# Gate, up and down products as unsplit fp32 matmuls in an attention and GEGLU kernel

## The chip, the cores and the metric

The kernel runs on one core of a Trainium2 chip. The metric is the device time of one execution, in microseconds (us); lower is better. Nothing else runs on the chip.

## What is computed

The input x has 2048 rows (tokens) of 576 columns. Its layer norm xn feeds two branches, self-attention with 32 heads of 18 columns, and a GEGLU feed-forward block with 4608 hidden columns; their outputs are multiplied, and x is added:

```python
xn = layernorm(x)
s  = attention(xn, wqkv, wo)                        # 32 heads, Dh = 18, softmax over 2048 keys
g  = silu((gelu(xn @ w_gate) * (xn @ w_up)) @ w_down)   # F = 4608, gelu with tanh
out = x + s * g
```

All inputs and the output are fp32.

## The kernel before, in words

**Numbers.** TensorE (PE) takes two kinds of 32-bit operand here: F32, and F32R, a 32-bit format that has been rounded. Every product but one is made with F32R operands. Where a product needs more than one rounded operand holds, each fp32 operand is cut in two: a high part (the rounded value) and a low part (the rest). A product is then three matmuls that add up in one PSUM bank: high by high, low by high, high by low. The one exception is the product of the softmax weights with the values (`values`, L764), whose operands are F32 and not split.

**Tiling of the feed-forward block.** The tokens go in NB = 4 blocks of 512, the hidden columns in 36 tiles of 128. One *section* (`section`, L533) is one token block by one hidden tile; there are NF = 144 of them. A section makes the transposed gate values `pg` and up values `pu`, each 128 hidden columns by 512 tokens, in one PSUM bank each. The 576 input columns are contracted in NC = 9 chunks of 64. Partitions 0 to 63 of the weight tile hold the gate weights, 64 to 127 the up weights, and the transposed xn (`xd`) lies twice, once in each half. So `pair` (L409) issues one matmul for `pg` in the upper 64 rows of the array and one for `pu` in the lower 64 rows, and there are 9 x 3 = 27 such pairs in a section (`terms`, L407).

**Activation.** `activate` (L423) makes gelu(pg) * pu: Square on ScalarE (ACT), a multiply on VectorE (DVE), a copy of `pu` to `t2` on ACT and `t2 * pg` on DVE (`times`), then tanh on ACT and (tanh + 1) * t2 on DVE (`rest`, L440). The last 6 sections (`early` false) use a shorter form without `t2`.

**Splits.** GpSimd (POOL) splits the weights of the next section, in three pieces of 128x384 (`split_gu`, L129), with `split` (L105: a tensor_scalar for the high part, a tensor_tensor for the low part). `finish` (L577) splits the hidden values into `hh` and `hl` and, in every second section, the w_down rows into `dh` and `dl`. In the first ten sections ACT makes the high part (`split_ap`), in the last six ACT and DVE split (`cut`). The transposed xn is split once, in `split_t` (L185), stored to DRAM as two arrays (`xhs`, L249), and loaded as `xd` (L142), after which POOL copies it to the other half of the partitions (L146).

**Down product.** Two hidden tiles (G = 2) make one *block* of the down product: 8 sums (4 token tiles of 128, by 2 column halves of 288), each over 256 hidden columns, that DVE adds to `Y` (`add_down`, L448). There are 72 blocks. In most of them (`half_downs`, L474) each 128-row product is cut into two halves of 64 rows; the rows 0 to 63 and 64 to 127 of the array work on different sums, and each half is one matmul of 64 rows (`down_product`, L463, L465), 6 terms per sum and half. The other blocks use 128 rows at once.

**Attention and the order of the work.** The order of PE's instructions is written out by hand (`manual_schedule` for PE); the other engines' are arranged by a scheduler, within the order of each tile's uses. Attention is cut into 32 units of 4 heads by 512 queries. In sections 10 to 137 the 27 gate and up pairs are interleaved (`spread`) with 16 pairs of attention matmuls: one score matmul `pe` (L729, then Exp on ACT, L730) and one matmul `pm` (L698) of a later unit for the row maximum (L699, DVE). Both have 64 rows, and the two of a pair take the two halves of the array. After every second section comes a burst of the value products (L764: 8 key tiles by 4 heads, 128 rows by 32 columns each, the four heads in the array's four column strips), and after the others a down block. Before the sections stand the layer norm, its transposes, and the query, key and value projections (L180, 128 rows, F32R, three terms); after section 137 the output projection (L902) runs with the last six sections.

Of the kernel before, what the change touches and what calls it, by code (L numbers as in the profile page):

```python
# [17 lines left out]
P = 128  # L18
# [29 lines left out]
BANKS = {"f": 2, "m": 3, "s": 3}  # L48
EPS = 1e-5
# [20 lines left out]
def kernel(ctx: ExitStack, tc: tile.TileContext, x, wqkv, wo, w_gate, w_up, w_down, out):  # L70
# [19 lines left out]
    xhs = [dram.tile([2, D, TB], F32, name=f"xhs{b}") for b in range(NB)]  # L90
# [28 lines left out]
    def raw_tile(shape, pool=wts):  # L119
        return pool.tile(shape, F32, name="raw", tag="raw", bufs=2)  # L120

    def load_gu(t, keep=lambda i: i):

        raw = raw_tile([P, NC, P])
        for a, w in enumerate((w_gate, w_up)):
            keep(nc.sync.dma_start(raw[HR * a:HR * a + HR], w[:, t * P:(t + 1) * P].rearrange("(k p) n -> p k n", p=HR)))
        return raw, [], []

    def split_gu(w, k, keep=lambda i: i):  # L129
        hi, lo = (wts.tile([P, XG, P], F32R, name=m, bufs=5) for m in ("wh", "wl"))  # L130
        first = split(hi, lo, w[0][:, XG * k:XG * k + XG, :], keep)
        w[1].append(hi)
        w[2].append(lo)
        return first

    def load_xd(b, key=None):

        xd = [[], []]
        for c in range(0, NC, XG):
            for i in range(2):  # L140
                t = wts.tile([P, XG, TB], F32R, name=f"xd{i}_{c}")
                asked[:] = [nc.sync.dma_start(f(t)[0:HR], xhs[b][i, c * HR:(c + XG) * HR, :]  # L142
                                              .rearrange("(k p) t -> p k t", p=HR))]
                if key:
                    no_sync(asked[0], key, "keys first")
                copied[:] = [nc.gpsimd.tensor_copy(t[HR:P], t[0:HR])]  # L146
                xd[i].append(t)
        return xd
# [8 lines left out]
    with tc.tile_pool(name="pro", bufs=1) as pro, tc.tile_pool(name="pps", bufs=1, space=PSUM) as pps:  # L157
# [27 lines left out]
        def split_t(pt, k, xt):  # L185

            if k < KT:
                nc.scalar.activation(xt[0][:, k, :], pt, AF.Copy)
# [45 lines left out]
        def transposes(b, xr):  # L234
            xt = XT[b % 2]
            pts = [pps.tile([P, TB], F32, name="pt", bufs=KT + 1) for k in range(KT + 1)]
            for j in range(4):
                if b == 0 and j == 0:
                    warm(46)
                for k in range(KT + 1):  # L240
                    nc.tensor.transpose(pts[k][:, j * P:(j + 1) * P], xr[j][:, k * P:(k + 1) * P], ident)  # L241
            for k in range(KT + 1):
                split_t(pts[k], k, xt)
            return xt

        def store_xt(b, xt):
            keep = tc.keep_in_program_order if b == 0 else lambda i: i
            for i in range(2):
                keep(nc.sync.dma_start(xhs[b][i, 0:R0, :].rearrange("(k p) t -> p k t", p=P), f(xt[i])))  # L249
                keep(nc.sync.dma_start(xhs[b][i, R0:D, :], f(xt[2])[HR * i:HR * i + HR, :]))  # L250
# [96 lines left out]
        for b in range(NB):  # L347
# [29 lines left out]
            if b == 2:  # L377
                ahead = load_gu(0, tc.keep_in_program_order)
                for k in range(NG):
                    split_gu(ahead, k)  # L380
# [22 lines left out]
    def gate_up(tag):  # L403

        w, xd = FF["w"], FF["xd"]
        pg, pu = (ps.tile([P, TB], F32, name=n, tag=tag, bufs=BANKS[tag]) for n in ("pg", "pu"))
        terms = [(wp, *divmod(c, XG), xp) for c in range(NC) for wp, xp in ((0, 0), (1, 0), (0, 1))]  # L407

        def pair(i):  # L409
            wp, k, c, xp = terms[i]  # L410
            for a, o in enumerate((pg, pu)):
                rr = slice(HR * a, HR * a + HR)
                nc.tensor.matmul(o, w[1 + wp][k][rr, c, :], xd[xp][k][rr, c, :], start=(i == 0),  # L413
                                 stop=(i == len(terms) - 1))

        return [lambda i=i: pair(i) for i in range(len(terms))], pg, pu
# [6 lines left out]
    def activate(pg, pu, early):  # L423

        t1 = ffn.tile([P, TB], F32, name="t1", bufs=2)
# [10 lines left out]
        def rest(behind=None, evicted=None):  # L436
            tanh = kept(nc.scalar.activation(t1, t1, AF.Tanh, scale=GC * GS))
            if behind:
                no_sync(tanh, behind, "a mark first")
            one = kept(nc.vector.scalar_tensor_tensor(t1, t1, 1.0, t2 if early else pg, op0=ALU.add, op1=ALU.mult))  # L440
            if evicted:
                no_sync(one, evicted, "a finished sum first")
            if not early:
                kept(nc.vector.tensor_tensor(t1, t1, pu, op=ALU.mult))
# [13 lines left out]
    DOWN = [(a, w, g) for g in range(G) for a, w in ((0, 0), (0, 1), (1, 0))]  # L458
# [4 lines left out]
    def down_product(py, hs, wd, j, c, i, rr=slice(0, P), start=False, stop=False):  # L463
        a, w, g = DOWN[i]
        return nc.tensor.matmul(py, hs[g][a][rr, j * P:(j + 1) * P], wd[w][rr, g, 288 * c:288 * c + 288],  # L465
                                start=start, stop=stop)
# [7 lines left out]
    def half_downs(b, r, hs, wd, Y):  # L474
# [9 lines left out]
        def downs_of(a, ks):  # L484
            for k in ks:
                for i in range(m):
                    def step(k=k, i=i):
# [6 lines left out]
                        one = down_product(pys[k], hs, wd, j, c, i, slice(HR * a, HR * a + HR), fresh,  # L494
                                           begun == 0 and i == m - 1)
                        if begun == 0 and i == 0 and k in seen:
                            after(one, seen[k])
# [31 lines left out]
    def load_down(r, raw):  # L529
        kept(nc.sync.dma_start(raw, w_down[r * G * P:(r + 1) * G * P, :].rearrange("(g p) n -> p g n", p=P)))  # L530
        return raw

    def section(specials=(), tag="f", raw_d=None, ahead=True):  # L533
# [17 lines left out]
        if nxt:  # L551
            for k in range(NG - 1 if ahead else 0):
                first = split_gu(nxt, k, kept)
                if k == 0 and n in ATT and n > ATT.start:
                    no_sync(first, FF["hl"], "hidden values first")
        if g == G - 1:
            FF["rawd"] = load_down(r, raw_d() if raw_d else raw_tile([P, G, D])) if ahead else FF.pop("next_d")
        for p in spread(pairs, specials):
            p()
        if nxt and ahead:  # L560
            split_gu(nxt, NG - 1, kept)
# [15 lines left out]
    def finish(pool=ffn, cut=split, bufs=1):  # L577
# [6 lines left out]
        if n in ATT and copied:  # L584
            no_sync(first, copied.pop(), "transposed x first")
        FF["hl"] = low_part[0]
        FF["hs"].append((hh, hl))
        if n % G == G - 1:
            wd = [pool.tile([P, G, D], F32R, name=m, bufs=bufs) for m in ("dh", "dl")]
            cut(*wd, FF["rawd"])  # L590
            for h in range(2):
                once = n in ATT and n + G in ATT
                FF["down"].append((b, r, FF["hs"], wd, FF["Y"], (2 * h, 2 * h + 1), once, n + 1 + (0 if once else h)))
# [51 lines left out]
    with tc.tile_pool(name="att", bufs=1, reuse_waits="tile") as att:  # L645
# [155 lines left out]
        def lead_raw():  # L801
            t = att.tile([P, QD, TB], F32, name="pT", bufs=8)
            return t.rearrange("p a t -> p (a t)")[:, 0:G * D].rearrange("p (g d) -> p g d", g=G)

# [7 lines left out]
        for n, m in enumerate(FIRST):  # L812
            none = [lambda: None]
            lead = [lambda s=s: lead_pair(s) for s in range(slot, slot + m)]
            section((n == 2) * 5 * none + lead + (m > 0 and n != 2) * none, "s" if n == 1 else "f", lead_raw)
# [12 lines left out]
            finish(cut=split_ap)  # L828
# [28 lines left out]
    with tc.tile_pool(name="epi", bufs=1, reuse_waits="tile") as epi:  # L857
# [57 lines left out]
        def cut(hi, lo, raw):  # L915
            split_av(hi, lo, raw, kept)

# [11 lines left out]
        def next_weights(n):  # L929


            if n + 2 < ENDS:
                FF["next_gu"] = load_gu((len(FIRST) + n + 2) % (NR * G), kept)
            if n % G == 0:
                FF["next_d"] = load_down((len(FIRST) + n) // G % NR, epi.tile([P, G, D], F32, name="raw", tag="raw"))

        done = 0
        for n in range(NU * NA, ENDS):
# [23 lines left out]
            else:  # L962
                next_weights(n)
                for k in range(0 if last else NG - 1):
                    split_gu(FF["w"], k, kept)
            downs()
            run_rest()
            if first or last:
                finish(epi, cut, 2)
            else:  # L970
                for i in range(3):
# [6 lines left out]
                    if i == 0:  # L978
                        split_gu(FF["w"], NG - 1, kept)
                    prepare(done - 1 + AHEAD)  # L980
                    if i == 1:
                        finish(epi, cut, 2)
# [59 lines left out]
```

## Time and profile before

| what | us |
|---|---|
| median of 3 runs | 2548.07 (2547.3 to 2548.31) |
| span of the profiled execution | 2545.4 |
| median less that span | 2.7 |
| PE busy | 2538.4 |
| DVE busy | 1950.4 |
| ACT busy | 1555.1 |
| POOL busy | 1320.7 |

The span runs from the first to the last recorded instruction. PE in the profile is TensorE's matmuls, PEld its weight loads, which run beside them. A matmul's record lasts until its last result has come out, so the records of matmuls that follow one another overlap, and so do those of two matmuls in the two halves of the array: the pace of PE is read from the distance of the starts, not from the length of a record. `x2592` in a row is the number of records.

### The profile page before, as it was taken

Reading aid. Unit: us, or ns where it says so; the run is one execution under the profiler, and the core shown is the slowest. Engines: PE = TensorE matmul, PEld = TensorE weight load, DVE = VectorE, ACT = ScalarE, POOL = GpSimd, SP = SyncE. Lnnn points to the kernel's source line nnn. Section 1 sums busy time; section 2 is a strip of 40 time slices with the busy share of each in tenths; the row PEclk is TensorE's granted clock in tenths of the full one; section 3 lists DMA queues with packets and bytes.
Section 4 is the critical chain, followed back from the end, with each engine's and each line's share of the span. In section 5 each row is a group of like instructions: output and inputs, shape, how many; then the busy total and the mean of one; then the engine's idle time right before and its main releaser. Section 6 shows DMA issues by size and latency. Waiting matters only on the chain.

```text
span 2545.4 us, 63167 instructions
## 1 busy us (share of the span) xinstructions
PE 2538.4 (100%) x23974; PEld 2008.4 (79%) x23974; DVE 1950.4 (77%) x3499; ACT 1555.1 (61%) x3050; POOL 1320.7 (52%) x1447
## 2 busy tenths in 40 slices
PE   9999999999999999999999999999999999999999
PEld 8888877777777777777777787777777777787798
DVE  5316988888888888888888888888888888887277
ACT  3223366666677666676666677666676666676612
POOL 2117545555465554445565545554446555455675
PEclk9999999999999999999999999999999999999999
DMA  8876444444465444444455444444446444444483
GB/s 267 269 241 158 100 103 106 100 111 109 107 150 121 104 109 112 113 112 110 111 125 140 116 111 106 105 108 112 109 109 153 115 109 109 108 106 99 114 242 107
DMA packets 398686, 325.51 MB, mean 128 GB/s; under 512 B 117408, under 2 KB 309184, under 8 KB 398384
## 3 DMA queue, kind: packets, MB, share of 16 engines
q1 hardware_dynamic: 398384, 321.47, 49.7%
q8 instruction: 191, 3.13, 0.5%
q14 instruction: 111, 0.91, 0.1%
HBM read 266.63 MB, written 54.70 MB: 126 GB/s over the span
## 4 chain that ended last, share of the span: by engine, by line
PE 98%; ACT 1%; DVE 0%; DMA 0%; SPq 0%; issue 0%; ACTq 0%
PE pg L413 29%; PE py L465 18%; PE acc L764 18%; PE pm L698 9%; PE pe L729 9%; PE po L180 7%; PE pu L413 6%; PE po L902 2%; ACT pT L730 1%; PE pt L241 0%; SPq L665 0%; DMA xx<-in_A_x_dram 0%; DVE bs L209 0%; ACT t L426 0%; DMA KS<-qk 0%
## 5 line engine op out<-in xcount | busy, mean ns | idle before, releaser
L730 ACT ACTIVATE pT<-pe 128x512 f32<-128x512 f32 x2048 | 1153.3, 598 | 368.7 <-PE pm L698 226.3
L699 DVE TENSOR_REDUCE mx<-pm 128x1 f32<-128x512 f32 x2048 | 1249.6, 680 | 151.3 <-PE pm L698 149.0
L413 PE MATMUL pg<-xd,wh 64*128 64x512 f32 x2592 | 928.9, 390 | 0.0
L413 PE MATMUL pu<-xd,wh 64*128 64x512 f32 x2592 | 928.6, 390 | 0.0
L698 PE MATMUL pm<-KS,q 64*128 64x512 f32 x2048 | 779.0, 388 | 0.8 <-DMA KS<-qk 0.5
L729 PE MATMUL pe<-q,KS 64*128 64x512 f32 x2048 | 775.2, 387 | 0.0
L413 PEld LDWEIGHTS pg<-xd,wh 64*128 64x128 f32 x2592 | 476.5, 184 | 115.9 <-POOL wh L106 21.1
L413 PE MATMUL pg<-xd,wl 64*128 64x512 f32 x1296 | 501.6, 387 | 0.0
L413 PE MATMUL pu<-xd,wl 64*128 64x512 f32 x1296 | 501.4, 387 | 0.0
L413 PEld LDWEIGHTS pu<-xd,wh 64*128 64x128 f32 x2592 | 477.0, 184 | 2.0
L764 PE MATMUL acc<-pT,VS 128*32 128x512 f32 x4096 | 452.8, 594 | 0.0
L108 POOL TENSOR_TENSOR wl<-raw,wh 128x384 fp32r<-128x384 f32 x432 | 434.2, 1019 | 13.7
L106 POOL TENSOR_SCALAR hh<-t 128x512 fp32r<-128x512 f32 x128 | 79.1, 618 | 652.0 <-DVE t L440 637.8
L698 PEld LDWEIGHTS pm<-KS,q 64*128 64x128 f32 x2048 | 374.2, 184 | 31.1 <-DVE mx L699 4.3
L729 PEld LDWEIGHTS pe<-q,KS 64*128 64x128 f32 x2048 | 370.9, 184 | 21.9
L465 PE MATMUL py<-dh,hh 64*128 64x288 f32 (+1 forms) x2160 | 360.3, 294 | 0.3
L465 PE MATMUL py<-dl,hh 64*128 64x288 f32 (+1 forms) x2160 | 358.7, 292 | 0.0
L465 PE MATMUL py<-dh,hl 64*128 64x288 f32 (+1 forms) x2160 | 358.3, 292 | 0.0
L764 PEld LDWEIGHTS acc<-pT,VS 128*32 128x32 f32 x4096 | 127.4, 110 | 289.9 <-issue 278.0
L106 POOL TENSOR_SCALAR wh<-raw 128x384 fp32r<-128x384 f32 x432 | 217.2, 515 | 143.7 <-PE pu L413 83.4
L453 DVE TENSOR_TENSOR Y<-py,Y 128x288 f32<-128x288 f32 x544 | 227.1, 452 | 59.8 <-PE py L465 52.7
L413 PEld LDWEIGHTS pg<-xd,wl 64*128 64x128 f32 x1296 | 238.7, 184 | 32.1
(119 smaller groups left out, 3106.7 us busy)
## 6 DMA issues: line engine op xcount, KB each, us to landing
KS<-qk SPq DMA_DIRECT2D x1536, 36.0 KB
raw<-in_B_w_gate_dram SPq DMA_DIRECT2D x144, 288.0 KB
raw<-in_B_w_up_dram SPq DMA_DIRECT2D x144, 288.0 KB
raw<-in_B_w_down_dram SPq DMA_DIRECT2D x67, 576.0 KB
VS<-vs SPq DMA_DIRECT2D x128, 152.0 KB
qk<-t SPq DMA_DIRECT2D x72, 256.0 KB
q<-qk SPq DMA_DIRECT2D x384, 36.0 KB
xx<-in_A_x_dram SPq DMA_DIRECT2D x32, 288.0 KB
```

Of the source, the lines that this page charges most:

```text
L106: first = nc.gpsimd.tensor_scalar(hi, raw, 1.0, 1.0, op0=ALU.mult, op1=ALU.mult)
L108: low_part[:] = [keep(nc.gpsimd.tensor_tensor(lo, raw, f(hi), op=ALU.subtract))]
L180: nc.tensor.matmul(o, st, m, start=(i == 0), stop=(i == len(terms) - 1))
L413: nc.tensor.matmul(o, w[1 + wp][k][rr, c, :], xd[xp][k][rr, c, :], start=(i == 0), stop=(i == len(terms) - 1))
L453: one = kept(nc.vector.tensor_tensor(yy, py, yy, op=ALU.add))
L465: return nc.tensor.matmul(py, hs[g][a][rr, j * P:(j + 1) * P], wd[w][rr, g, 288 * c:288 * c + 288], start=start, stop=stop)
L698: nc.tensor.matmul(pm, QS[u, r][rr, t * P:(t + 1) * P], KS[(u * NA + c) % KB][r][rr, :], start=True, stop=True)
L699: nc.vector.tensor_reduce(MX[u][:, 2 * r + a, t, c:c + 1], pm, axis=AX.X, op=ALU.max)
L729: nc.tensor.matmul(pe, KS[(u * NA + c) % KB][r][rr, t * P:(t + 1) * P], QS[u, r][rr, :], start=True, stop=True)
L730: nc.scalar.activation(PT[u, kt][:, 2 * r + a, :], pe, AF.Exp, scale=SCALE)
L764: nc.tensor.matmul(ACC[u][32 * a:32 * a + 32, :], VS[(u * NA + c) % VB][:, v:v + 32], pt[:, a, :], start=first, stop=last, skip_group_chec ...
L902: nc.tensor.matmul(po, parts_of(b, j)[x_][:, k, :], OW[w][c][k], start=(i == 0), stop=(i == len(OUT) - 1))
```

## The change

The operands of the gate, up and down products are no longer split. The weights are loaded as fp32 (`gu`, three buffers, and `wd`, three buffers) and used as they are; the hidden values go from the activation (`t1`, now four buffers) to the down product; the transposed xn is kept whole, in a third copy that ACT makes in the prologue (`xf`), stored to DRAM as one array and loaded as `xd`. Each product that was three matmuls with F32R operands is one matmul with F32 operands, of the same 64 rows, 128 stationary columns and 512 or 288 moving columns. The loops over `CW` have one pass, since `CW` is 128. The gelu of sections 0 to 137 ends on POOL, in two instructions, where it ended on DVE in one. Some orders written by hand that belonged to the splits go. Attention and the projections keep their F32R operands and splits.

```diff
+CW = P
-    xhs = [dram.tile([2, D, TB], F32, name=f"xhs{b}") for b in range(NB)]
+    xhs = [dram.tile([D, TB], F32, name=f"xhs{b}") for b in range(NB)]
...
     def load_gu(t, keep=lambda i: i):
-        raw = raw_tile([P, NC, P])
+        t_ = wts.tile([P, NC, P], F32, name="gu", bufs=3)
...
-    def split_gu(w, k, keep=lambda i: i):
...
     def load_xd(b, key=None):
-        xd = [[], []]
+        xd = []
         for c in range(0, NC, XG):
-            for i in range(2):
-                t = wts.tile([P, XG, TB], F32R, name=f"xd{i}_{c}")
...
+            t = wts.tile([P, XG, TB], F32, name=f"xd{c}")
...
-        def split_t(pt, k, xt):
+        def split_t(pt, k, xt, xf):
+            if k < KT:
+                nc.scalar.activation(xf[:, k, :], pt, AF.Copy)
+            else:
+                nc.scalar.activation(xf[0:HR, k, :], pt[0:HR], AF.Copy)
...
+        XF = [pro.tile([P, KT + 1, TB], F32, name="xf")] * 2
...
-        terms = [(wp, *divmod(c, XG), xp) for c in range(NC) for wp, xp in ((0, 0), (1, 0), (0, 1))]
-        def pair(i):
-            wp, k, c, xp = terms[i]
-            for a, o in enumerate((pg, pu)):
-                rr = slice(HR * a, HR * a + HR)
-                nc.tensor.matmul(o, w[1 + wp][k][rr, c, :], xd[xp][k][rr, c, :], start=(i == 0),
-                                 stop=(i == len(terms) - 1))
+        def pair(c):
+            for o in range(0, P, CW):
+                for a, out_ in enumerate((pg, pu)):
+                    rr = slice(HR * a, HR * a + HR)
+                    nc.tensor.matmul(out_[o:o + CW, :], w[rr, c, o:o + CW], xd[c // XG][rr, c % XG, :], start=(c == 0),
+                                     stop=(c == NC - 1), skip_group_check=True)
...
-        t1 = ffn.tile([P, TB], F32, name="t1", bufs=2)
+        t1 = ffn.tile([P, TB], F32, name="t1", bufs=G + 2)
...
-            one = kept(nc.vector.scalar_tensor_tensor(t1, t1, 1.0, t2 if early else pg, op0=ALU.add, op1=ALU.mult))
...
+            if early:
+                kept(nc.gpsimd.tensor_scalar(t1, t1, 1.0, 1.0, op0=ALU.add, op1=ALU.mult))
+                kept(nc.gpsimd.tensor_tensor(t1, t1, t2, op=ALU.mult))
+            else:
+                kept(nc.vector.scalar_tensor_tensor(t1, t1, 1.0, pg, op0=ALU.add, op1=ALU.mult))
...
-    DOWN = [(a, w, g) for g in range(G) for a, w in ((0, 0), (0, 1), (1, 0))]
+    DOWN = list(range(G))
...
-        a, w, g = DOWN[i]
-        return nc.tensor.matmul(py, hs[g][a][rr, j * P:(j + 1) * P], wd[w][rr, g, 288 * c:288 * c + 288],
-                                start=start, stop=stop)
+        for o in range(0, P, CW):
+            one = nc.tensor.matmul(py[o:o + CW, :], hs[i][rr, j * P + o:j * P + o + CW], wd[rr, i, 288 * c:288 * c + 288],
+                                   start=start, stop=stop, skip_group_check=True)
+            first = one if o == 0 else first
+        return first, one
...
-        hh = ffn.tile([P, TB], F32R, name="hh", bufs=G + 1)
-        hl = ffn.tile([P, TB], F32R, name="hl", bufs=G + 1)
-        first = cut(hh, hl, FF["act"])
...
+        FF["hs"].append(FF["act"])
         if n % G == G - 1:
-            wd = [pool.tile([P, G, D], F32R, name=m, bufs=bufs) for m in ("dh", "dl")]
-            cut(*wd, FF["rawd"])
```

More of the change, by code (lines that the diff above doesn't have):

```diff
@@ L117, in split_av, with raw_tile @@
         keep(nc.vector.tensor_tensor(lo, raw, f(hi), op=ALU.subtract))
-    def raw_tile(shape, pool=wts):
-        return pool.tile(shape, F32, name="raw", tag="raw", bufs=2)
+    def raw_tile(shape):
+        return wts.tile([P, NC, P], F32, name="gu", bufs=3).rearrange("p k n -> p (k n)")[:, 0:shape[1]]
     def load_gu(t, keep=lambda i: i):
-        raw = raw_tile([P, NC, P])
+        t_ = wts.tile([P, NC, P], F32, name="gu", bufs=3)
         for a, w in enumerate((w_gate, w_up)):
-            keep(nc.sync.dma_start(raw[HR * a:HR * a + HR], w[:, t * P:(t + 1) * P].rearrange("(k p) n -> p k n", p=HR)))
-        return raw, [], []
-    def split_gu(w, k, keep=lambda i: i):
[L130 to L134, printed above, removed]
+            keep(nc.sync.dma_start(t_[HR * a:HR * a + HR], w[:, t * P:(t + 1) * P].rearrange("(k p) n -> p k n", p=HR)))
+        return t_
     def load_xd(b, key=None):
-        xd = [[], []]
+        xd = []
         for c in range(0, NC, XG):
-            for i in range(2):
-                t = wts.tile([P, XG, TB], F32R, name=f"xd{i}_{c}")
[L142 to L147, printed above, removed]
+            t = wts.tile([P, XG, TB], F32, name=f"xd{c}")
+            asked[:] = [nc.sync.dma_start(t[0:HR], xhs[b][c * HR:(c + XG) * HR, :].rearrange("(k p) t -> p k t", p=HR))]
+            if key:
+                no_sync(asked[0], key, "keys first")
+            copied[:] = [nc.gpsimd.tensor_copy(t[HR:P], t[0:HR])]
+            xd.append(t)
         return xd
@@ L406, in gate_up @@
         pg, pu = (ps.tile([P, TB], F32, name=n, tag=tag, bufs=BANKS[tag]) for n in ("pg", "pu"))
[L407 to L416 removed]
+        def pair(c):
[4 more added lines that the diff above has]
+                                     stop=(c == NC - 1), skip_group_check=True)
+        return [lambda c=c: pair(c) for c in range(NC)], pg, pu
     def gate(o, th, yy):
@@ L493, in step @@
                         begun = a if k < low else 1 - a
-                        one = down_product(pys[k], hs, wd, j, c, i, slice(HR * a, HR * a + HR), fresh,
+                        first, one = down_product(pys[k], hs, wd, j, c, i, slice(HR * a, HR * a + HR), fresh,
                                            begun == 0 and i == m - 1)
                         if begun == 0 and i == 0 and k in seen:
-                            after(one, seen[k])
+                            after(first, seen[k])
                         if i == m - 1:
@@ L527, in down, with load_down, section @@
                 kept(nc.sync.dma_start(ys[b * TB + j * P:b * TB + (j + 1) * P, :], Y[:, j]))
[L529 to L533, printed above, removed]
+    def load_down(r):
+        wd = wts.tile([P, G, D], F32, name="wd", bufs=3)
+        kept(nc.sync.dma_start(wd, w_down[r * G * P:(r + 1) * G * P, :].rearrange("(g p) n -> p g n", p=P)))
+        return wd
+    def section(specials=(), tag="f", ahead=True):
         n = FF["n"]
@@ L551, in section @@
         if nxt:
[L552 to L555, printed above, removed]
+            pass
         if g == G - 1:
-            FF["rawd"] = load_down(r, raw_d() if raw_d else raw_tile([P, G, D])) if ahead else FF.pop("next_d")
+            FF["rawd"] = load_down(r) if ahead else FF.pop("next_d")
         for p in spread(pairs, specials):
             p()
-        if nxt and ahead:
-            split_gu(nxt, NG - 1, kept)
         FF["w"] = nxt
@@ L575, in downs, with finish @@
             down(*FF["down"].pop(0)[:-1])
-    def finish(pool=ffn, cut=split, bufs=1):
+    def finish():
         n = FF["n"] - 1
         b, r = divmod(n // G, NR)
-        hh = ffn.tile([P, TB], F32R, name="hh", bufs=G + 1)
-        hl = ffn.tile([P, TB], F32R, name="hl", bufs=G + 1)
-        first = cut(hh, hl, FF["act"])
[L584 to L587, printed above, removed]
+        FF["hs"].append(FF["act"])
         if n % G == G - 1:
-            wd = [pool.tile([P, G, D], F32R, name=m, bufs=bufs) for m in ("dh", "dl")]
-            cut(*wd, FF["rawd"])
             for h in range(2):
                 once = n in ATT and n + G in ATT
-                FF["down"].append((b, r, FF["hs"], wd, FF["Y"], (2 * h, 2 * h + 1), once, n + 1 + (0 if once else h)))
+                FF["down"].append((b, r, FF["hs"], FF["rawd"], FF["Y"], (2 * h, 2 * h + 1), once, n + 1 + (0 if once else h)))
     def load_numbers(num, rb, g, toks):
@@ L814 @@
             lead = [lambda s=s: lead_pair(s) for s in range(slot, slot + m)]
-            section((n == 2) * 5 * none + lead + (m > 0 and n != 2) * none, "s" if n == 1 else "f", lead_raw)
+            section((n == 2) * 5 * none + lead + (m > 0 and n != 2) * none, "s" if n == 1 else "f")
             if slot + m >= NS > slot:
@@ L827 @@
             downs()
-            finish(cut=split_ap)
+            finish()
         for n in range(NU * NA):
@@ L934, in next_weights @@
             if n % G == 0:
[L935 removed]
+                FF["next_d"] = load_down((len(FIRST) + n) // G % NR)
         done = 0
@@ L968 @@
             if first or last:
-                finish(epi, cut, 2)
+                finish()
             else:
```

23 lines of the change are left out of this document (4 added, 19 removed).

## The prediction, made before the changed kernel ran

> **What bounds the kernel now.** I read the page first: busy times, then the chain that ended last. In the busy rows each engine is followed by its time, its share of the span and its number of instructions; the chain gives shares of the span.
>
> ```profile
> PE 2538.4 (100%) x23974; PEld 2008.4 (79%) x23974; DVE 1950.4 (77%) x3499; ACT 1555.1 (61%) x3050; POOL 1320.7 (52%) x1447
> PE 98%; ACT 1%; DVE 0%; DMA 0%; SPq 0%; issue 0%; ACTq 0%
> ```
>
> PE is busy throughout and is 98% of the chain. Matmul records overlap, so this could still hide slack; the pace has to be read from starts. The timeline of one stretch in the middle (start, length, engine, line, operation) gives it; the cut-out rows go on in the same way:
>
> ```profile
> 1300.20 0.39 PE L729 MATMUL pe<-q,KS 64*128 64x512 f32 x1
> 1300.20 0.39 PE L698 MATMUL pm<-KS,q 64*128 64x512 f32 x1
> 1300.43 0.39 PE L413 MATMUL pg<-xd,wh 64*128 64x512 f32 x1
> 1300.43 0.39 PE L413 MATMUL pu<-xd,wh 64*128 64x512 f32 x1
> ...
> 1307.00 0.39 PE L413 MATMUL pg<-xd,wh 64*128 64x512 f32 x1
> 1307.00 0.39 PE L413 MATMUL pu<-xd,wh 64*128 64x512 f32 x1
> 1307.23 0.29 PE L465 MATMUL py<-dh,hh 64*128 64x288 f32 x2
> ...
> 1312.00 0.29 PE L465 MATMUL py<-dh,hh 64*128 64x288 f32 x2
> ```
>
> Two matmuls of 64 rows start together, one in each half of the array. From 1300.20 to 1307.23 there are 31 such starts: 7.03 / 31 = **0.227 us per pair** with 512 moving columns. From 1307.23 to 1312.00 there are 36 steps: 4.77 / 36 = **0.1325 us per pair** with 288. Starts follow without holes, so here PE works at its own pace; neither ACT nor DVE holds it up.
>
> Now the counts, from the groups (records, then busy and mean ns; the other two terms of each down form have the same counts):
>
> ```profile
> L413 PE MATMUL pg<-xd,wh 64*128 64x512 f32 x2592 | 928.9, 390 | 0.0
> L413 PE MATMUL pg<-xd,wl 64*128 64x512 f32 x1296 | 501.6, 387 | 0.0
> L465 PE MATMUL py<-dh,hh 64*128 64x288 f32 x2016 | 315.8, 293 | 0.2
> L465 PE MATMUL py<-dh,hh 128*128 128x288 f32 x144 | 44.5, 309 | 0.1
> L764 PE MATMUL acc<-pT,VS 128*32 128x512 f32 x4096 | 452.8, 594 | 0.0
> ```
>
> Gate and up: 2592 + 1296 = 3888 pairs x 0.227 = 883 us. Down in halves: 3 x 2016 = 6048 matmuls, 3024 pairs x 0.1325 = 401 us. Down with 128 rows, which I take at the same pace (mean 309 against 293 ns): 432 x 0.1325 = 57 us. These 1341 us are what the change touches, and PE is the bound in all of it.
>
> **What an unsplit fp32 matmul costs: the term that decides.** The trace has one product of this kind, the value products at L764. The program has 32 units x 16 key tiles x 4 heads = 2048 of them, and the trace 4096 records: each fp32 matmul is *two* records, each with a weight load of its own. One burst:
>
> ```profile
> 1323.47 7.07 PE L764 MATMUL acc<-pT,VS 128*32 128x512 f32 x64
> ```
>
> It holds 64 records = 16 sets of four (four heads, in four column strips side by side). The last set ends 0.59 us after its start (mean of the row above), so a set takes (7.07 - 0.59) / 15 = **0.432 us**, close to twice a pair of the F32R kind (0.227). A record is thus two passes over its 512 columns and a matmul four, 2 x 0.432 = **0.864 us**, where the three F32R terms take 3 x 0.227 = **0.681 us**. One matmul for three is four passes for three.
>
> No record of 64 rows by 128 columns in fp32 exists in this trace. Bounds: below, the burst's rate, 0.864 per pair; above, four F32R passes with the F32R overhead in each, 4 x 0.227 = 0.908. I take 0.864, because the burst is the row with the same operands. For 288 columns: 0.864 x 288 / 512 = 0.486 below, 4 x 0.1325 = 0.530 above; I take 0.486.
>
> **Do the halves still work side by side?** F32R pairs do (same start above). With two records a matmul there is a new question, that of order: in the compiled program the two records of a matmul stand one directly behind the other, first `pg`'s two, then `pu`'s two. The second must wait for the first in its half. If it held up everything behind it, the four heads' eight records would come in steps, two at a time, and 64 records would take about 33 x 0.432 = 14 us. The burst took 7.07: a strip goes on by itself while another is occupied. I expect the same of row halves, but no row shows it. Here a rule speaks against me: the Trainium skill, TensorE: Matmul & The Clock Gate, section "The mechanism" (Part 3), says that matmuls start and end in program order, "strict FIFO, no reordering". By that rule the burst would have taken the 14 us; the trace's 7.07 us disagrees for column strips. For row halves it becomes a rival below.
>
> **The sum.** Pairs after: 3888 / 3 = 1296 of gate and up, 3024 / 3 = 1008 of down halves, 432 / 3 = 144 with 128 rows.
> - Gate and up: 1296 x (0.864 - 0.681) = +237 us (upper bound, 0.908: +294).
> - Down halves: 1008 x (0.486 - 0.3975) = +89 us (upper, 0.530: +134).
> - Down, 128 rows: 144 x 0.0885 = +13 us (upper +19).
> Together **+339 us**, upper bound +447.
>
> **The splits that go, and the gelu that moves.** They lie on engines off the chain:
>
> ```profile
> L108 POOL TENSOR_TENSOR wl<-raw,wh 128x384 fp32r<-128x384 f32 x432 | 434.2, 1019 | 13.7
> L106 POOL TENSOR_SCALAR wh<-raw 128x384 fp32r<-128x384 f32 x432 | 217.2, 515 | 143.7 <-PE pu L413 83.4 <-DMA raw<-in_B_w_up_dram 55.6 <-PE pm L698 3.4
> L108 POOL TENSOR_TENSOR hl<-t,hh 128x512 fp32r<-128x512 f32 x128 | 164.7, 1287 | 10.7
> L106 POOL TENSOR_SCALAR hh<-t 128x512 fp32r<-128x512 f32 x128 | 79.1, 618 | 652.0 <-DVE t L440 637.8 <-PE py L465 13.8
> L440 DVE SCALAR_TENSOR_TENSOR t<-t,t 128x512 f32<-128x512 f32 x138 | 97.3, 705 | 16.1 <-ACT t L437 2.0
> ```
>
> POOL sheds these 434 + 217 + 165 + 79 = 895 us and more, and gains 138 x (0.618 + 1.287) = 263 us by the durations of the same shapes. Nothing on the chain waits for POOL, so I cost both at 0 us. The cover is a whole section (over 10 us) between the end of a gelu and the down block that uses it; the new end takes 1.9 us where L440 and the split took 0.7 + 1.9. DVE loses L440's 97 us. One window over a whole period (two sections, a burst, a down block) shows the room; the columns are PE, PEld, DVE, ACT and POOL busy, each with its number of instructions:
>
> ```profile
> 1300.00:1333.50 33.50, 33.50 (x338) 26.00 (x336) 27.12 (x48) 23.27 (x47) 20.70 (x20) 1.00 0.71 152
> ```
>
> PE fills 33.5 of 33.5; DVE 27.1, ACT 23.3. The period grows by 18 x 0.183 + 16 x 0.0885 = 4.7 us, to 38.2, while DVE goes down to 25.7. The attention matmuls now come in bursts, two pairs (0.45 us) between two gate pairs (0.86): DVE's and ACT's share, at most two reductions or Exps of about 0.6 to 0.7 us per 1.32 us, still fits, with three banks for each. If it doesn't always, some tenths of a us per section over 128 sections, up to 40 us, are lost; the upper bound has room for it.
>
> **Prologue and DMA.** ACT makes five more copies for each token block:
>
> ```profile
> L188 ACT ACTIVATE xth<-pt 128x512 fp32r<-128x512 f32 x16 | 8.3, 604 | 2.6 <-PE pt L241 2.6
> ```
>
> 5 x 0.604 = 3 us. In the first block they stand ahead of the first projection: +3 us. In the other three they run beside the value projections on PE, whose three banks could run full: 0 to 3 us each. The single `xf` buffer makes the copies of the next block wait for the store of the last, 0 to 3 us. The end of the kernel has no split of the last hidden values: -1 us. I take +5 us in all (0 to 15). `xhs` and `xd` move half the bytes, the weights the same; SP issues fewer DMAs, and weights come a section ahead into three buffers. No chain step is a DMA: 0 us.
>
> Span 2545.4 + 339 + 5 = 2889 us. The median lay 2.7 us above the span: **2892 us**. Likeliest case with its bounds: 2870 to 3015 (+447, +15, rounded up).
>
> **Rivals.**
> 1. *Strict order between the halves.* A gate pair then takes steps: `pg` record 1 at 0, `pg` 2 and `pu` 1 at 0.432, `pu` 2 at 0.864, the attention matmul of the upper half at 0.864, that of the lower half only at 1.296, and what follows is behind it: 1.296 in place of 0.864 + 0.227 = 1.091, so +0.205 us. 9 pairs x 128 sections: +236 us; the ends of the 63 down blocks and of the other sections +20. Down pairs in a row cost nothing more. 2892 + 256 = **3148 us**. For: the program's order. Against: the burst.
> 2. *The halves take turns in fp32.* A pair costs 1.728 and a down pair 0.972: 1296 x 1.047 + 1008 x 0.5745 + 13 = +1949, **4502 us**. Against: F32R halves and fp32 strips both work side by side.
> 3. *Faster: a record of 64 rows needs one pass.* If the two passes come from the use of all 128 rows (the burst's form), a half-height matmul would cost 0.432 per pair: 1296 x (0.432 - 0.681) + 1008 x (0.243 - 0.3975) + 13 = -466, **2088 us**, with DVE (1950 - 97 = 1853 us) just below PE. It turns faster where a record costs under 0.34 us. Against: in F32R the number of rows makes little difference (mean lengths 293 and 309 ns in the two down rows above).
> 4. *The change saves waits that I don't see.* PE's starts follow without holes, so there is nothing to save; a result within 0.2% would need this to cancel 340 us.
>
> **How the numbers follow.** 0.2% is about what a measurement of this kernel can tell from no change. Likeliest case 0.73; rival 1 0.16; rival 2 0.04; rival 3 0.03; rival 4 0.01; slower for another reason, between 3015 and 3400 us, 0.03. The range reaches from below the likeliest case to rival 1: 2860 to 3155. Faster 0.03, same 0.01, slower 0.96.
>
> **What would show it.** 5184 records at the gate and up line (2592 matmuls, two each), with starts 0.43 to 0.45 us apart in each half, and mean lengths near 0.59 us as in the burst; down records 0.24 to 0.27 us apart. Between a gate pair and the next attention pair 0.86 to 0.9 us, both attention matmuls starting together; under rival 1 they start 0.43 us apart. PE still 98% of the chain; POOL's busy time under 750 us. Wrong would be: a PE with holes behind POOL or ACT, or a record length near 0.39 us (one pass).

## The result, and the profile after

The changed kernel took 2888.35 us (median of 4 runs, 2885.88 to 2889.15), the one before 2547.69 us (4 runs): a ratio of 1.1334, 95% interval 1.1318 to 1.135. It is 341 us slower. The forecast was 2892 us. The profiled execution has a span of 2884.1 us, 338.7 us more than before.

From the page of the changed kernel, the busy row and the chain by engine and by line:

```profile
PE 2873.3 (100%) x19222; PEld 1673.8 (58%) x19222; DVE 1936.2 (67%) x3352; ACT 1532.4 (53%) x3046; POOL 408.0 (14%) x448
PE 99%; DMA 0%; ACT 0%; DVE 0%; issue 0%; SPq 0%
PE pg L406 38%; PE py L459 19%; PE acc L748 16%; PE pe L713 9%; PE pm L682 8%; PE po L172 6%; PE po L882 2%; PE pu L406 1%; PE pt L237 0%; DMA rawp<-in_A_wqkv_dram 0%; DMA xhs<-xf 0%; ACT xf L180 0%; ACT xth L184 0%; DMA xx<-in_A_x_dram 0%; DVE bs L205 0%; DVE t L287 0%
```

The chain by line before:

```profile
PE pg L413 29%; PE py L465 18%; PE acc L764 18%; PE pm L698 9%; PE pe L729 9%; PE po L180 7%; PE pu L413 6%; PE po L902 2%; ACT pT L730 1%; PE pt L241 0%; SPq L665 0%; DMA xx<-in_A_x_dram 0%; DVE bs L209 0%; ACT t L426 0%; DMA KS<-qk 0%
```

PE is still the whole chain. POOL went from 1320.7 to 408.0 us, and nothing of that can be seen in the time. The chain's share of `pg` and `pu` rose from 35% to 39% of a longer span, from about 890 to about 1125 us. The shares are rounded to whole per cents, so this shows where the time went and is too coarse for a sum.

The groups of PE by form, with records, busy time and mean ns:

```profile
L406 PE MATMUL pg<-xd,gu 64*128 64x512 f32 x2592 | 1307.6, 589 | 0.0
L682 PE MATMUL pm<-KS,q 64*128 64x512 f32 x2048 | 1086.5, 607 | 0.0
L459 PE MATMUL py<-wd,t 64*128 64x288 f32 x4032 | 499.2, 402 | 0.0
L748 PE MATMUL acc<-pT,VS 128*32 128x512 f32 x4096 | 452.7, 594 | 0.0
L459 PE MATMUL py<-wd,t 128*128 128x288 f32 x288 | 74.3, 412 | 0.0
```

2592 records for `pg` are 1296 matmuls with two records each, as for the value products; the mean length, 589 ns, is that of the value products (594). There were 3888 `pg` records of 390 and 387 ns before. A trap lies in the second row: the attention matmul `pm` is the same as before, when its row was

```profile
L698 PE MATMUL pm<-KS,q 64*128 64x512 f32 x2048 | 779.0, 388 | 0.8 <-DMA KS<-qk 0.5 <-DVE mx L699 0.3
```

yet its mean length rose from 388 to 607 ns. It costs no more. Its record begins while the gate matmul ahead of it in the same half still runs. (The ends of matmul records are modelled by the profiler; that is one more reason to read the pace from starts.) The timeline of one step shows it:

```profile
1300.93 0.59 PE L406 MATMUL pg<-xd,gu 64*128 64x512 f32 x1
1300.93 0.59 PE L406 MATMUL pu<-xd,gu 64*128 64x512 f32 x1
1301.35 0.59 PE L406 MATMUL pg<-xd,gu 64*128 64x512 f32 x1
1301.36 0.59 PE L406 MATMUL pu<-xd,gu 64*128 64x512 f32 x1
1301.38 0.79 PE L713 MATMUL pe<-q,KS 64*128 64x512 f32 x1
1301.38 1.02 PE L682 MATMUL pm<-KS,q 64*128 64x512 f32 x2
1302.02 0.39 PE L713 MATMUL pe<-q,KS 64*128 64x512 f32 x1
1302.25 0.59 PE L406 MATMUL pg<-xd,gu 64*128 64x512 f32 x1
1302.25 0.59 PE L406 MATMUL pu<-xd,gu 64*128 64x512 f32 x1
```

Both halves start together, twice, 0.43 us apart: two records, read as two passes each, for one pair. Then come two attention pairs, and the next gate pair starts 1.32 us after the first. That is 0.86 + 2 x 0.23, so nothing is lost between the halves. (The prediction's sign, 0.86 us from a gate pair to the attention pair, can't be read directly: the attention records begin 0.45 us after the gate pair, for the reason just given.)

A down block now has 64 records in place of 96; the second row is the next work on PE:

```profile
1512.50 7.92 PE L459 MATMUL py<-wd,t 64*128 64x288 f32 x64
1520.04 0.61 PE L713 MATMUL pe<-q,KS 64*128 64x512 f32 x1
```

32 sets of two in 7.92 us, the last 0.40 us long: (7.92 - 0.40) / 31 = 0.2426 us a set, 0.485 per pair.

The span by stage, from the starts of the first gate matmul, the first score and the last score:

| stage | before, us | after, us | difference |
|---|---|---|---|
| prologue, to the first gate matmul | 196.2 | 203.4 | +7.2 |
| first sections, to the first score | 103.6 | 122.7 | +19.1 |
| attention sections (64 periods) | 2110.2 | 2406.8 | +296.6 |
| last sections and end | 135.5 | 151.2 | +15.7 |

A period of two sections, a burst and a block went from 32.97 to 37.61 us: +4.64.

### The profile page after: what moved, and what is told of

Read it like the earlier page. It is cut to its first block, busy times and chain, and to the rows that moved or that the text cites. A ratio compares the mean times of both kernels' runs of the same rounds, so it can differ in the third digit from the quotient of the medians.

```text
span 2884.1 us, 52436 instructions
## 1 busy us (share of the span) xinstructions
PE 2873.3 (100%) x19222; PEld 1673.8 (58%) x19222; DVE 1936.2 (67%) x3352; ACT 1532.4 (53%) x3046; POOL 408.0 (14%) x448
## 4 chain that ended last, share of the span: by engine, by line
PE 99%; DMA 0%; ACT 0%; DVE 0%; issue 0%; SPq 0%
PE pg L406 38%; PE py L459 19%; PE acc L748 16%; PE pe L713 9%; PE pm L682 8%; PE po L172 6%; PE po L882 2%; PE pu L406 1%; PE pt L237 0%; DMA rawp<-in_A_wqkv_dram 0%; DMA xhs<-xf 0%; ACT xf L180 0%; ACT xth L184 0%; DMA xx<-in_A_x_dram 0%; DVE bs L205 0%; DVE t L287 0%
## 5 line engine op out<-in xcount | busy, mean ns | idle before, releaser
L406 PE MATMUL pg<-xd,gu 64*128 64x512 f32 x2592 | 1307.6, 589 | 0.0
L406 PE MATMUL pu<-xd,gu 64*128 64x512 f32 x2592 | 1306.8, 589 | 0.0
L682 PE MATMUL pm<-KS,q 64*128 64x512 f32 x2048 | 1086.5, 607 | 0.0
L713 PE MATMUL pe<-q,KS 64*128 64x512 f32 x2048 | 1081.7, 610 | 0.0
L406 PEld LDWEIGHTS pg<-xd,gu 64*128 64x128 f32 x2592 | 479.0, 186 | 181.0 <-issue 87.8
L459 PE MATMUL py<-wd,t 64*128 64x288 f32 (+1 forms) x4320 | 573.5, 403 | 0.0
L459 PEld LDWEIGHTS py<-wd,t 64*128 64x128 f32 (+1 forms) x4320 | 437.4, 187 | 153.9 <-issue 41.6
L406 PEld LDWEIGHTS pu<-xd,gu 64*128 64x128 f32 x2592 | 480.2, 186 | 1.6
L420 DVE SCALAR_TENSOR_TENSOR t<-t,pg 128x512 f32<-128x512 f32 x144 | 98.8, 686 | 140.8 <-ACT t L419 140.7
L435 POOL TENSOR_TENSOR t<-t,t 128x512 f32<-128x512 f32 x138 | 175.4, 1271 | 11.5
```

What stands on the lines that cost most here:

```text
L406: nc.tensor.matmul(out_[o:o + CW, :], w[rr, c, o:o + CW], xd[c // XG][rr, c % XG, :], start=(c == 0), stop=(c == NC - 1), skip_group_check ...
L420: kept(nc.vector.scalar_tensor_tensor(t1, t1, 1.0 / GC, pg, op0=ALU.add, op1=ALU.mult))
L435: kept(nc.gpsimd.tensor_tensor(t1, t1, t2, op=ALU.mult))
L459: one = nc.tensor.matmul(py[o:o + CW, :], hs[i][rr, j * P + o:j * P + o + CW], wd[rr, i, 288 * c:288 * c + 288], start=start, stop=stop, s ...
L682: nc.tensor.matmul(pm, QS[u, r][rr, t * P:(t + 1) * P], KS[(u * NA + c) % KB][r][rr, :], start=True, stop=True)
L713: nc.tensor.matmul(pe, KS[(u * NA + c) % KB][r][rr, t * P:(t + 1) * P], QS[u, r][rr, :], start=True, stop=True)
```

## The experiments

The theory: a product costs its passes through PE, four for an fp32 matmul against three for the three F32R terms; all else that the change moves is hidden, but for some microseconds in the prologue. The rivals: part of the 341 us is waits (POOL's longer gelu, the third copy, new buffers), or part of it is order between the halves of the array. Each run stood beside runs of the kernel before on the same chip (2547 to 2548 us in all of them).

### Gate and up alone

On the changed kernel, the down product split again:

```diff
-        FF["hs"].append(FF["act"])
+        cut(hh, hl, FF["act"])
+        FF["hs"].append((hh, hl))
...
+            cut(*wd, FF["rawd"])
...
-    DOWN = list(range(G))
+    DOWN = [(a, w, g) for g in range(G) for a, w in ((0, 0), (0, 1), (1, 0))]
```

> Gate and up unsplit as in the changed kernel, the down product split into three F32R terms as before. Theory (four passes for three, all else hidden): the changed kernel's 2888 us less the down part, 1008 x 0.0885 + 144 x 0.0885 = 102 us, so 2786 us (2775 to 2800); the splits of the hidden values after the gelu on POOL stay hidden. Rival (a part of the 340 us is not matmul passes but waits behind POOL's gelu or the new buffers): the time does not come out as that difference; with POOL's gelu and splits in one chain before the down block it would stay near 2888 us or above.

Measured: 2790.79 us (ratio to before 1.0955, 1.0938 to 1.0971), +243 us. The theory's 2786 missed by 5 us; the long chain on POOL, gelu and splits one after the other, cost no more than that.

### Down alone

On the kernel before, the hidden values and w_down unsplit:

```diff
-        FF["hs"].append((hh, hl))
+        FF["hs"].append(FF["act"])
...
-    DOWN = [(a, w, g) for g in range(G) for a, w in ((0, 0), (0, 1), (1, 0))]
+    DOWN = list(range(G))
```

> The kernel before with the down product alone unsplit; gate, up, xn and the end of the gelu as before. Theory: 2548 + 102 = 2650 us (2640 to 2660). Rival (waits): the two parts done alone, this one and gate and up alone, would not add up to the whole 340 us; if order between the halves cost something in the down blocks, this one would be over 2700 us.

Measured: 2638.95 us (1.0361, 1.0345 to 1.0376), +92 us, 10 less than worked out. The two parts give 243 + 92 = 335 of the 341 us: no large cost needs both.

### The end of the gelu back on DVE

```diff
-                kept(nc.gpsimd.tensor_scalar(t1, t1, 1.0, 1.0, op0=ALU.add, op1=ALU.mult))
-                kept(nc.gpsimd.tensor_tensor(t1, t1, t2, op=ALU.mult))
+                kept(nc.vector.scalar_tensor_tensor(t1, t1, 1.0, t2, op0=ALU.add, op1=ALU.mult))
```

> The changed kernel with the end of the gelu back on DVE, one instruction as before. Theory: POOL's two instructions were off the path and DVE has room (1936 us busy, +97): 2888 us, within 5 us. Rival (the longer end on POOL delays down blocks): faster by 10 us or more.

Measured: 2889.38 us (2886.8 to 2891.03) against 2888.35. No difference: the move to POOL neither cost nor brought anything here. The attention sections take 2406.8 us in both traces.

### No third copy of xn

```diff
-                nc.scalar.activation(xf[:, k, :], pt, AF.Copy)
...
-            keep(nc.sync.dma_start(xhs[b][0:R0, :].rearrange("(k p) t -> p k t", p=P), XF[b % 2][:, 0:KT, :]))
+            keep(nc.sync.dma_start(xhs[b][0:R0, :].rearrange("(k p) t -> p k t", p=P), f(xt[0])))
```

> The changed kernel without the third copy of xn: the high part of xn, which the projections use, is stored and loaded in its place, so the low part of xn is left out of gate and up. Theory: the copies cost about 5 us in the prologue, so 2883 us (2875 to 2887). Rival (the copies were hidden): 2888 us, no difference.

Measured: 2881.97 us (2881.27 to 2882.55), 6.4 us faster than the changed kernel by the medians. In the two traces the first gate matmul starts at 199.8 us in place of 203.4, 3.6 us earlier, and all later stages agree within 0.1 us. So the copies cost some 4 to 6 us, in the prologue.

### Four F32R terms

On the kernel before, a fourth term:

```diff
-        terms = [(wp, *divmod(c, XG), xp) for c in range(NC) for wp, xp in ((0, 0), (1, 0), (0, 1))]
+        terms = [(wp, *divmod(c, XG), xp) for c in range(NC) for wp, xp in ((0, 0), (1, 0), (0, 1), (1, 1))]
...
-    DOWN = [(a, w, g) for g in range(G) for a, w in ((0, 0), (0, 1), (1, 0))]
+    DOWN = [(a, w, g) for g in range(G) for a, w in ((0, 0), (0, 1), (1, 0), (1, 1))]
```

> The kernel before with a fourth term, low by low, in the gate, up and down products: four F32R matmuls where the changed kernel has one F32 matmul. Theory (a product costs its passes, 0.227 and 0.1325 us per F32R pair): +294 + 134 + 19 = 447 us, 2995 us (2970 to 3010), about 107 us above the changed kernel, whose passes have the smaller overhead of the value products (0.858 us per four). Rival (the price of the changed kernel is not one of passes): no such relation; near 2888 us if an F32 matmul were four F32R passes to the nanosecond.

Measured: 2983.69 us (1.1714, 1.1695 to 1.1734), +437 us where 447 were worked out. With all splits made and the order of the kernel before, a fourth F32R matmul alone costs more than the whole change. So the price of passes is enough to explain the change, and four F32R matmuls cost 95 us more than one fp32 matmul in the two kernels. That a record of an fp32 matmul is two passes is a reading of its time (0.429 us against 0.227); the trace shows records, not passes.

### Down matmuls grouped by half, two and four at a time

On the changed kernel, in `half_downs`, with K = 2 and K = 4:

```diff
-        for i, both in enumerate(zip(*rows, strict=True)):
-            for half in both if i < low * m + m else both[::-1]:
-                half()
+        for i in range(0, len(rows[0]), K):
+            for row in rows if i < low * m + m else rows[::-1]:
+                for half in row[i:i + K]:
+                    half()
```

> The changed kernel; in the down blocks two matmuls (four records) of one half are issued, then two of the other, where they alternated one by one. Theory (a half goes on by itself, records of one half do not hold up those of the other): 2888 us, within 10 us. Rival (records start in program order, so a record that waits for its own half holds up the other): a group of four takes 6 x 0.243 = 1.46 us in place of 0.97, 63 blocks x 8 groups x 0.49 = +245 us, 3130 us.

> As the run by two, but four matmuls (eight records) of one half, then four of the other. Theory: 2888 us, within 15 us, if PE can look eight records and their weight loads ahead; if its look ahead is shorter, some tenths of the rival's price. Rival (program order): 14 x 0.243 = 3.4 us per group in place of 1.94, 63 x 4 x 1.46 = +367 us, 3255 us.

Measured: by two 2901.99 us, +14 us; by four 3094.31 us (1.2147 of before), +206 us. The down records in the first two stretches of 0.97 us of a down block (length, PE busy, granted clock, DMA share and GB/s; the number behind x counts the records that run in the stretch, and in the first stretch all of them also start there), by two:

```profile
1521.28:1522.25 0.97, 0.96 (x8) 1.00 0.28 78
1522.25:1523.22 0.97, 0.97 (x11) 1.00 0.22 76
```

and by four:

```profile
1532.04:1533.01 0.97, 0.96 (x4) 1.00 0.33 112
1533.01:1533.98 0.97, 0.97 (x9) 1.00 0.19 61
```

By two, four records of the one half stand ahead of the first of the other, and still eight start in the first stretch, both halves at once. By four, eight stand ahead, and only four start: the other half begins when the fifth record of the first half does. So neither of the two theories holds alone. The halves are independent as long as few records of one stand ahead of the other: four ahead cost 14 us in all, 0.22 us for each of the 63 blocks, and eight cost 206 us, 3.3 us a block (the rival's program order: 245 and 367 us). In the changed kernel it is two. What sets the limit, records or their weight loads, was not tested.

### Fewer columns per matmul

On the changed kernel:

```diff
-CW = P
+CW = 64
```

and, in a second run, `CW = 32`.

> The changed kernel with each product as two matmuls of 64 stationary columns (64 rows by 64 columns, four corners of the array). Theory (the four corners work side by side, each with four passes): 2888 us, within 20 us. Rival (only halves of rows work side by side, or the doubled number of records costs something each): up to double, 1296 x 0.86 + 1008 x 0.49 = +1600 us.

> The changed kernel with each product as four matmuls of 32 stationary columns (eight tiles of the array). Theory (as with four column strips in the value products, at 0.43 us per record): 2888 us, within 30 us, if PE can hold 16 records and their weight loads per chunk in flight. Rival (look ahead too short, or a cost per record): slower by 7 ns or more for each of the 31000 added records, +200 us or more.

Measured: 3298.01 us with 64 columns and 3303.38 with 32, +410 and +415 us. My expectation was wrong. The timeline of the run with 64 columns, from one gate step to the next:

```profile
1510.73 0.64 PE L406 MATMUL pg<-xd,gu 64*64 64x512 f32 x1
...
1511.21 0.59 PE L406 MATMUL pg<-xd,gu 64*64 64x512 f32 x1
...
1511.75 0.50 PE L682 MATMUL pm<-KS,q 64*128 64x512 f32 x1
...
1512.41 0.64 PE L406 MATMUL pg<-xd,gu 64*64 64x512 f32 x1
```

A step takes 1.68 us in place of 1.32, and a down block in the same run takes what it did:

```profile
1502.43 7.94 PE L459 MATMUL py<-wd,t 64*64 64x288 f32 x128
1510.30 0.50 PE L713 MATMUL pe<-q,KS 64*128 64x512 f32 x1
```

7.94 us against 7.92, with twice the records, and 7.97 us in the run with 32 columns, with four times as many. So the four corners do work side by side, as do eight tiles. The theory now: the cost comes where the shape of the tiles changes, between the gate pairs (64 by 64) and the attention pairs (64 by 128). 9 x 128 = 1152 such places at 1.68 - 1.32 = 0.36 us would be 415 us. That is a little too much: the attention sections of the two traces differ by 397 us, mostly because the steps that hold a burst of value products grow by only 0.17 us (the tile shape changes there in any case). This theory got a run of its own: 64 columns in the down products only.

```diff
-CW = P
+CW = 64
...
-            for o in range(0, P, CW):
+            for o in range(0, P, P):
                 for a, out_ in enumerate((pg, pu)):
...
-                    nc.tensor.matmul(out_[o:o + CW, :], w[rr, c, o:o + CW], xd[c // XG][rr, c % XG, :], start=(c == 0),
+                    nc.tensor.matmul(out_[o:o + P, :], w[rr, c, o:o + P], xd[c // XG][rr, c % XG, :], start=(c == 0),
```

> The changed kernel with the down products alone in 64 columns (four corners), gate and up with 128. Theory (the 410 us of the run with 64 columns everywhere come at the changes of the array's shape between gate pairs and attention pairs, 1152 places of about 0.36 us; down blocks change shape only at their two ends): 2888 us plus 63 blocks x 0.36, at most 2915 us. Rival (a cost per record of 64 columns): the down blocks' 4032 added records carry 4032 / 9200 of the 410 us, +180 us.

Measured: 2911.87 us, +23.5 us, or 0.37 us for each of the 63 blocks, where a cost per record would have been +180 us. The change of shape is the cause; a cost per record as the main part is ruled out.

### The high term alone

On the kernel before, to see what lies behind PE:

```diff
-        terms = [(wp, *divmod(c, XG), xp) for c in range(NC) for wp, xp in ((0, 0), (1, 0), (0, 1))]
+        terms = [(wp, *divmod(c, XG), xp) for c in range(NC) for wp, xp in ((0, 0),)]
...
-    DOWN = [(a, w, g) for g in range(G) for a, w in ((0, 0), (0, 1), (1, 0))]
+    DOWN = [(0, 0, g) for g in range(G)]
```

> The kernel before with the high by high term alone in the gate, up and down products; the splits are still made, the two other terms are left out, so the result lacks the low parts. It shows what bounds the kernel once PE has less to do. Theory: PE loses 2592 x 0.227 + 2016 x 0.1325 + 288 x 0.1325 = 893 us, which would be 1655 us; DVE, 1950 us busy before, becomes the bound: 2000 to 2150 us. Rival (PE's chain stays the bound whatever the passes): 1655 us.

Measured: 2421.62 us (0.9507, 0.9488 to 0.9526), 126 us faster than before and not the 400 to 550 I expected. The busy row and the chain:

```profile
PE 2222.9 (92%) x14470; PEld 1286.6 (53%) x14470; DVE 1946.9 (80%) x3499; ACT 1489.7 (62%) x3050; POOL 1348.2 (56%) x1447
DVE 50%; PE 30%; POOL 6%; DMA 5%; SPq 4%; issue 2%; ACT 2%; POOLq 0%; DVEq 0%; ACTq 0%
```

DVE is the bound in half of the span, above all in the sections, where it takes the row maxima (38% of the chain); in the bursts of value products (14%) and the projections (7%) it is PE. I had set the whole span to the busier engine; the bound changes from stage to stage, and so the times of the stages add up to more than either engine's.

The same on the changed kernel, with the gelu's end on POOL, where it now matters:

```diff
+        hi = wts.tile([P, NC, P], F32R, name="wh", bufs=2)
+        kept_r[0](nc.gpsimd.tensor_scalar(hi, t, 1.0, 1.0, op0=ALU.mult, op1=ALU.mult))
...
-                kept(nc.gpsimd.tensor_tensor(t1, t1, t2, op=ALU.mult))
+                kept(nc.gpsimd.tensor_tensor(tr, t1, t2, op=ALU.mult))
...
+            wd = ffn.tile([P, G, D], F32R, name="dh", bufs=2)
+            kept(nc.gpsimd.tensor_scalar(wd, FF["rawd"], 1.0, 1.0, op0=ALU.mult, op1=ALU.mult))
```

> The high by high term alone, as the one-term run, but built on the changed kernel: weights only rounded on POOL, the hidden values rounded by the gelu's last instruction, which stays on POOL, no third copy of xn, no low parts made; the result lacks the low parts. In the one-term run DVE is 50% of the chain and 1947 us busy. Theory (a move from DVE to POOL is worth something only where DVE is on the path): DVE loses 97 us and some of POOL's waits go, 2422 less 60 to 130 us, 2290 to 2360 us. Rival (the longer end of the gelu or the rounding on POOL is on the path now): no gain, 2422 us or more.

Measured: 2356.58 us (0.9252, 0.9237 to 0.9267), 65 us less than the other one-term kernel, within the range. Its busy row and chain:

```profile
PE 2181.9 (93%) x14470; PEld 1261.6 (54%) x14470; DVE 1806.1 (77%) x3352; ACT 1470.7 (62%) x3026; POOL 656.7 (28%) x664
DVE 44%; PE 34%; DMA 6%; POOL 4%; issue 4%; ACT 4%; SPq 4%; POOLq 0%; ACTq 0%; DVEq 0%
```

DVE's busy time fell by 141 us, its share of the chain from 50% to 44%. The run changes more than the gelu, so the 65 us are not the gelu's alone. Both one-term kernels beat the other two in time, but they compute less: the low parts are missing.

## Why the prediction was right

- **What bounds the kernel: right.** PE was 98% of the chain and is 99%. POOL shed 913 us of work for nothing, and the run with the gelu's end on DVE agrees.
- **The price of an unsplit matmul: right within 1%.** Taken: 0.864 us per pair from the burst of value products; measured 0.858 (starts 0.429 us apart, the median over the run). The upper bound, 0.908, was the price of four F32R passes, and the run with four terms shows that kernel at 2984 us (2995 worked out).
- **Halves side by side, in any order of their records: right, with a limit that I did not know.** Rival 1's step of 1.296 us between a gate pair and what follows the attention pair does not appear: the next gate pair starts 1.32 us after the last one, with two attention pairs in between, where rival 1 gives 1.296 + 0.227 = 1.52. The Trainium skill's rule that matmuls start in program order ("TensorE: Matmul & The Clock Gate", section "The mechanism") fails here for row halves too, in the run by two; in the run by four, something like it begins after four records.
- **The sum: right, with some us in the wrong terms.** Gate and up were put at +237. At the measured pace the pairs come to 1296 x (0.858 - 0.681) = +229. The run with that part alone gave +243, of which 9 lie ahead of its first gate matmul (205.6 us against 196.2 in the traces); so about 5 us behind it are not explained by the pace. Down +102: alone +92, though its pairs are as priced (0.485 against 0.486 us). About half of the missing 10 us can be seen: from the first to the last start, the 63 down blocks of the attention sections took 6.232 us at best and 6.318 in the mean before, and 7.518 us each in that run. So the blocks of the kernel before had lost 5.4 us that the unsplit form does not lose; rival 4's waits existed, at that size. What they waited for, and the other half, stays open. The third copy and the prologue, put at +5: 7.2 us between the two traces, but the first gate matmul of the eight kernels with this prologue starts anywhere from 202.9 to 207.4 us, so this term is known to some 2 us only. With the measured pace and prologue the sum is 229 + 102 + 7 = 338 us, and the spans differ by 338.7. The two parts alone missed their sums by about +5 and -10 us, so that the whole fits to 1 us, and the forecast to 4, is in part luck.
- **The cover: right.** DVE and ACT kept up with the attention pairs that now come two at a time; a period grew by 4.64 us, and 4.7 were worked out. (The 33.5 us that the prediction started from was the length of its window; the period was 32.97 us.) The allowance of up to 40 us for PSUM waits was not needed.
- **Rivals 2 and 3** (halves in turn; one pass per record) are excluded by the starts: both halves start together, and their records follow 0.43 us apart.

## What to carry to other kernels

Where TensorE is the bound, count passes: by the times here, an fp32 matmul made four where three F32R terms made three, and nearly everything that the simpler form saved on other engines was time that nobody waited for. Price a form that the kernel doesn't use yet by the one product in the trace that does, record by record, and check against the pace of starts, not against record lengths. Keep neighbours on TensorE in one tile shape: 64 rows by 64 columns beside 64 by 128 cost 0.36 us per change there and back.

## What the runs showed of the hardware that was not expected

- The change of tile shape: 0.36 to 0.37 us for there and back, 397 us in all at the 1152 places of the attention sections, and next to nothing inside a run of equal tiles (7.94 us for 128 records of 64 columns, 7.92 for 64 records of 128). The Trainium skill says that changing the tiling mode drains TensorE ("TensorEngine Tiling (Array Packing)", section "Key Properties"); the runs agree in that such a change costs time, and add the price; a drain as such is not seen in them. The price depends on the shapes: in the kernel before, a burst of value products (128 by 32) between pairs of 64 by 128 starts 0.315 us after the pair ahead of it, where 0.227 is the pace, and the next pair starts 0.543 us after the last set of the burst, where 0.432 is the pace, so 0.2 us for there and back.
- The two halves may run apart, but not far: with four records of one half ahead in the program both started at once, and the kernel lost 14 us; with eight ahead the other half started 0.97 us late, and the kernel lost 206 us.
- Half a record of an fp32 matmul over 512 columns took 0.2145 us (0.429 / 2), a whole F32R record 0.227, in 64 rows by 128 columns both.
- In the one-term run, where PE was busy for 92% of the span, the mean granted clock was 0.96 in place of 1.00. What that cost was not measured by itself.
